# Routed attention and a hard-swish layer on one core: mask product in front, weight sums made earlier, loads issued later

## The chip, the core and the metric

The kernel runs on one core of one Trainium2 chip. The core has five engines that run side by side, each through its own list of instructions: TensorE (PE in the profile) for matrix products, VectorE (DVE), ScalarE (ACT) and GpSimd (POOL) for element-wise work, and SyncE (SP), which here only issues transfers. The metric is the device time of one execution in microseconds (us); the lower the better.

## The reference

Two layers follow one another. The first is attention in which a query sees only the keys of its own cluster; the second is a two-layer network with a hard-swish between.

```python
# q, k, v: (4, 8, 768, 64) float32; centroids: (8, 16, 64)
q_assign = np.argmax(np.einsum('bhsd,hcd->bhsc', q_n, c_n), axis=-1)
k_assign = np.argmax(np.einsum('bhsd,hcd->bhsc', k_n, c_n), axis=-1)
mask = q_assign[:, :, :, None] == k_assign[:, :, None, :]
scores = scale * np.matmul(q, k.transpose(0, 1, 3, 2))
scores = np.where(mask, scores, -1000000000.0)
attn = softmax(scores); attn_out = np.matmul(attn, v)
# x: (4*768, 512), heads side by side
h = x @ w_in                      # w_in (512, 2048), float64
g = h * np.clip(h + 3.0, 0.0, 6.0) / 6.0
out = g @ w_out                   # w_out (2048, 512), float64
```

Here `q_n`, `k_n` and `c_n` are the rows divided by their lengths.

## The kernel before, in words

The kernel is one program with a hand-written order. Attention works on 16 pairs of heads (g = 0 to 15). A pair has 12 items: an item is one block of 128 keys (j = 0 to 5) against half of the queries (hf = 0 or 1). The number n counts items over all pairs, 192 in all, and `where(n)` gives pair, half and key block. The big loop steps n by two, so that a step r = 0, 2, ... 10 of a pair takes two items. Four pairs make a batch.

**Scores (lines 410 to 429).** The scores of an item lie in a PSUM tile `ps`, of which there are two. For each head t of the pair, one f32 product of keys and queries from `xf` uses 64 rows of the array, so the two heads run side by side on rows 0 to 63 and 64 to 127. Then a second product from `xm` adds the mask: `xm` holds the one-hot cluster vectors of queries and, times a large negative number, the complement for keys, in bf16, so that items of different clusters get a large negative score. `scores` writes the f32 product first and the mask product after it. ScalarE then takes the exponential into `ex` (line 434), GpSimd sums the keys (`acc`), and PE multiplies by the values (`pv`, line 467).

**Preparing the next pair.** During pair g the queries and keys of pair g + 1 are turned by PE (`turn`), assigned to clusters (`cluster_scores`, `route`), and the one-hot vectors turned into `xm` (`route_turn`). At step r = 6 the loop issues the loads of q and k of pair g + 2 and of v of pair g + 1 (lines 873 to 875), six transfers of 192 KB on the Sync queue. A transfer there is issued only after those in front of it.

**From one by one to four by four.** For the first 96 items every step does all its work alone. From item 96 on (`fours`) the scores of four items, or of two, are taken together, and at r = 2, 6 and 10 a batch of the second layer's items (`fill`) is taken off a list, mixed with the preparing of the next pair (lines 876 to 883).

**The second layer (`ffn_items`).** Its tokens come in 12 blocks of 256. A block has 8 items `up` (the first product, with two of the 16 column tiles of `w_in` each) and 7 items `down` (the second product, parts 0 to 6). The first block's `up` is done plainly (line 603). All other blocks do the first product by a Strassen-like scheme with seven smaller products instead of eight (`halved`, tiles `uX` and `uY`): it needs three sums of weight tiles, called `tx`, and changes one weight tile of `w_in_sb` in place. VectorE adds the parts up into `g_sb`. The second product uses the same scheme from the first block on, with its own sums T1 to T4.

**Where `tx` comes from (`first_sums`, line 560).** u counts the `up` items over all blocks. For the second block (u = 8 to 15) VectorE makes the sums by four subtractions of 128x256 elements and a transfer stores them in HBM as `td`. For all later blocks a transfer reads them back from `td`. There are three buffers for `tx`. The call is two items ahead: `up` item u calls `first_sums(u + 2)`; the sums for u = 8 and 9 are made in parts 5 and 6 of the first block's `down` (lines 714 and 715).

**The Sync queue** carries, in the order of the program, loads of q, k and v, stores of the attention's result `num` to `xd` (line 496, which waits for VectorE's division), loads of token blocks `xb`, stores to `td`, reads of `tx`, and stores of the output.

Of the kernel before, what the change touches and what calls it, by code (L numbers as in the profile page):

```python
# [8 lines left out]
F32 = mybir.dt.float32  # L9
# [3 lines left out]
ALU = mybir.AluOpType  # L13
# [103 lines left out]
def fast_path(ctx, tc, ok, q, k, v, centroids, moe_w_in, moe_w_out, out):  # L117
# [288 lines left out]
    def where(n):  # L406
        g, r = divmod(n, 2 * NCH)
        return (g, *divmod(r, NCH))

    def scores_qk(n):  # L410
        g, hf, j = where(n)
        st["ps", n] = psum_s.tile([P, 2, 512], F32, name="ps")
        scores_part(n, st["xf", g], True)

    def scores_part(n, x, first):
        g, hf, j = where(n)
        for t in range(2):
            r = slice(t * D, (t + 1) * D)
            nc.tensor.matmul(  # L419
                st["ps", n][:, t, 0:HALF], lhsT=x[r, NCH + j],  # L420
                rhs=x[r, hf * NHC : (hf + 1) * NHC], start=first,
                stop=not first or by_vector(n),
            )

    def scores(n):
        if ("ps", n) not in st:
            scores_qk(n)
        if not by_vector(n):
            scores_part(n, st["xm", where(n)[0]], False)

    def exponentials(n):
        sc = st.pop(("ps", n))[:, :, 0:HALF]
# [127 lines left out]
    def first_sums(u):  # L560

        blk, i = divmod(u, HF)
        if not 0 < blk < B * NHC:
            return
        tx = st["tx", u] = txp.tile([P, 3, HK, P], F32, name="tx")
        if blk == 1:
            t1, t2, t4 = (tx[:, k] for k in range(3))
            b11, b12, b21, b22 = wi(0, 0, i), wi(0, 1, i), wi(1, 0, i), wi(1, 1, i)
            for out_, in0, in1 in ((t1, b12, b11), (t2, b22, t1), (t4, b21, t2), (b12, b22, b12)):
                nc.vector.tensor_tensor(out=out_, in0=in0, in1=in1, op=ALU.subtract)  # L570
            nc.sync.dma_start(td[:, i], tx)
        else:
            nc.sync.dma_start(tx, td[:, i])

    def token_sums(b, m):

# [15 lines left out]
    def ffn_items(b):  # L592
        def up(m, i):
            def item():
                load_block()
                u = (b * NHC + m) * HF + i
                g = g_sb[:, 0:4, i]
                if u < HF:
                    ph = psum_m.tile([P, 512], F32, name="ph", tag="m")
                    for t in range(2):  # L600
                        f = t * HF + i
                        for kt in range(NKT):
                            nc.tensor.matmul(  # L603
                                ph[:, t * HC : (t + 1) * HC], lhsT=w_in_sb[:, kt, f * P : (f + 1) * P],
                                rhs=st["xb", b, m][:, kt], start=(kt == 0), stop=(kt == NKT - 1),
                            )
                    ph = ph.rearrange("p (k c) -> p k c", k=4)
                    lift(g, ph)
                    clip(g, g, ph)
                    gated_sums(i)  # L610
                else:
                    halved(b, m, u, i, g)
                if u >= HF or i < HF - 2:
                    first_sums(u + 2)
                if i == HF - 1:
                    st.pop(("xb", b, m)), st.pop(("xs", b, m), None)
                    st["free"] = True
                    load_block()
                    finish()

            return item
# [70 lines left out]
        def down(m, part):  # L692
            def item():
                if part == 0:
                    st["X"] = psum_m.tile([P, DM], F32, name="X", tag="m")
                    st["y0"] = yp.tile([P, DM], F32, name="y0", tag="y0")
                elif part == 2:
                    st["Y"] = psum_m.tile([P, DM], F32, name="Y", tag="m")
                    st["y1"] = yp.tile([P, DM], F32, name="y1", tag="y1")

                if part < 2:
                    h = range(part * HF // 2, (part + 1) * HF // 2)
                    product(st["X"], 0, 0, wb[0][0], True, False, False, h)
                    product(st["X"], 1, 5, st["T2"], False, True, False, h)
                kind, bank, half, w = (
                    None, None,
                    (4, "Y", 0, st["T1"]), (1, "Y", 1, st["T3"]),
                    (2, "X", 0, wb[1][0]), (6, "Y", 0, wb[1][1]), (3, "Y", 1, st["T4"]),
                )[part] or (None,) * 4
                if part > 1:  # L710
                    product(st[bank], half, kind, w, part == 2, part in (3, 4, 6), part > 3)
                if part == 4:
                    token_sums(*divmod(b * NHC + m + 1, NHC))
                if (b, m) == (0, 0) and part > 4:
                    first_sums(HF + part - 5)
                y0, y1 = st["y0"], st.get("y1")
                if part == 1:
                    nc.scalar.copy(out=y0[:, HC:], in_=st["X"][:, HC:])
                    add(y0[:, HC:], y0[:, HC:], st["X"][:, 0:HC])
                elif part == 3:  # L720
                    add(y1[:, 0:HC], y0[:, HC:], st["Y"][:, HC:])
                    add(y1[:, HC:], y1[:, 0:HC], st["Y"][:, 0:HC])
                elif part == 4:
                    nc.scalar.copy(out=y0[:, 0:HC], in_=st["X"][:, 0:HC])
                elif part == 6:
                    add(y1[:, 0:HC], y0[:, HC:], st["Y"][:, HC:])
                    nc.sync.dma_start(out_v[b, 2 * m + 1], y1)
                    add(y0[:, HC:], y0[:, HC:], st["Y"][:, 0:HC])
                    nc.sync.dma_start(out_v[b, 2 * m], y0)

            return item
# [99 lines left out]
    with tc.manual_schedule():  # L831
        nc.scalar.dma_start(cen, centroids.rearrange("h c d -> (h c) d"))
        load(0, "q", "k")
        constants()
        load(0, "v")
        load_weights(0)
        centroid_norm()
        for part in range(3):
            turn(0, part)
        centroid_turn()  # L840
        nc.vector.tensor_copy(out=ident_q, in_=ident)
        load(1, "q", "k")
        cluster_scores(0)
        scores_qk(0)
        route(0)
        scores_qk(1)
        for part in range(2):
            route_turn(0, part)

        for n in range(0, total + lag_d + 2, 2):  # L850
            g, r = divmod(n, per_pair)
            fours = n >= DECODED
            steps = [i for i in (n, n + 1) if i < total]
            prep = prep_items(g + 1, r, fours)
            if fours:
                four_by_four(n, r, steps)
            else:
                for i in steps:
                    scores(i)
                    exponentials(i)  # L860
                    key_sums(i)
                for i in (n - lag_v, n - lag_v + 1):
                    if i >= 0:
                        attn_v(i)
                m = n - lag_d + 1
                if m >= 0 and m % NCH == NCH - 1:
                    later.append(divide(m))
                    ready(m)
            if prep and r == (6 if fours else 4):
                prep.pop(0)()  # L870
            if n == DECODED:
                st["early"] = False
            if r == 6:
                load(g + 2, "q", "k")
                load(g + 1, "v")
            if not fours or r % 4 == 2 or n >= total:
                want = min(items_by(n + 2) - st["done"], len(fill))
                st["done"] += want
                for i in range(max(len(prep), want)):
                    if i < want:  # L880
                        fill.pop(0)()
                    if i < len(prep):
                        prep[i]()
            for step in decode[: share[r]]:
                step()
            del decode[: share[r]]
            if not fours:
                for op in numbers:
                    op()
                numbers.clear()  # L890
                check_all()
            checks.extend(later)
            later.clear()

        while checks:
            check_all()
            checks.extend(later)
            later.clear()
        st["last"] = True
        for item in fill:  # L900
            item()
# [385 lines left out]
```

## Time and profile before

| | |
|---|---|
| device time, median of 3 runs | 1033.52 us (1029.15 to 1035.98) |
| span of the profiled execution | 1024.4 us |
| exponentials, ACT, x192 | 148.4 us, 806 ns each |
| score products, PE, 768 records | 165.5 us of PE's time |
| mask products, PE, 384 records | 63.1 us of PE's time |
| reads of `tx`, x80, 384 KB each | 3.2 us from issue to landing |
| loads of q and of k, x32 each, 192 KB | 4.3 and 4.6 us from issue to landing |

The profile records every instruction of one execution. An f32 matmul shows as two records, so that the scores of an item are four records of `ps<-xf` and two of `ps<-xm`. Records of PE overlap, since the two heads run side by side and matmuls are pipelined: busy time is the union of the records, and what a group costs is read best from the distance between starts. A row of the timeline gives start, length, engine, line, operation, output and inputs, the shape, the count, and in brackets the idle time before it with what ended it. "PEld" is the loading of weights, "SPq" the Sync queue. A row of waits gives who waited for whom, the sum in us, how often, and the longest.

### The profile page before, as it was taken

What the parts mean: (1) busy time and instruction counts of PE and PEld (TensorE: products, weight loads), DVE (VectorE), ACT (ScalarE), POOL (GpSimd) and SP (SyncE); (2) the same over time, 40 slices, a digit from 0 to 9 for tenths busy, and PEclk for the clock granted to TensorE, in tenths of its full rate; (3) what the DMA queues carried; (4) which work ended last, traced back from release to release, by engine and by line L of the source; (5) the groups of instructions that cost most, each with busy time, mean ns of one, the idle gap of its engine ahead of it and who ended that gap; (6) DMA issues with size and microseconds to landing.
All of it is one profiled execution on the core that took longest, in us unless ns stands there. A gap on an engine that the chain in (4) does not pass through costs nothing.

```text
span 1024.4 us, 16727 instructions
## 1 busy us (share of the span) xinstructions
PE 997.8 (97%) x6560; PEld 738.4 (72%) x6560; DVE 562.8 (55%) x1085; ACT 390.0 (38%) x764; POOL 433.3 (42%) x363
## 2 busy tenths in 40 slices
PE   8999999999999999999999999999999999999996
PEld 4444445546778777778787777678787898999995
DVE  4899977868368245226336236227246272727270
ACT  6888876675233233233323333333223020202010
POOL 4777756766325426426415415524516230303030
PEclk9999999999999999999999999999999999999999
DMA  6355664532223222223224025023023051414120
GB/s 177 101 145 144 165 165 97 143 86 46 58 91 110 55 91 83 54 75 103 58 83 118 27 68 152 9 70 98 29 84 97 3 154 40 143 40 126 51 63 25
DMA packets 107176, 90.34 MB, mean 88 GB/s; under 512 B 78416, under 2 KB 88656, under 8 KB 107088
## 3 DMA queue, kind: packets, MB, share of 16 engines
q1 hardware_dynamic: 106944, 89.15, 31.1%
q8 instruction: 54, 0.88, 0.3%
q14 instruction: 34, 0.28, 0.1%
q10 hardware_dynamic: 144, 0.03, 0.0%
HBM read 73.43 MB, written 15.73 MB: 87 GB/s over the span
## 4 chain that ended last, share of the span: by engine, by line
PE 84%; ACT 4%; DVE 4%; DMA 4%; SPq 2%; issue 1%; POOL 0%; ACTq 0%; DVEq 0%; POOLq 0%
PE Y L683 16%; PE uY L648 14%; PE ps L419 12%; PE X L683 12%; PE uX L648 11%; PE pv L467 9%; PE ph L603 3%; SPq L195 2%; PE pd L488 2%; PE pqk L310 2%; DMA raw<-in_moe_w_in_dram 1%; ACT ex L434 1%; PE pcs L323 1%; DMA tx<-td 1%; DVE wunit L247 1%
## 5 line engine op out<-in xcount | busy, mean ns | idle before, releaser
L457 POOL TENSOR_TENSOR acc<-acc,ex 128x768 f32<-128x768 f32 x128 | 241.3, 1885 | 139.0 <-ACT ex L434 132.6
L638 POOL TENSOR_TENSOR g_sb<-g_sb 128x256 f32<-128x256 f32 x176 | 130.5, 763 | 325.9 <-DVE g_sb L519 322.5
L434 ACT ACTIVATE ex<-ps 128x768 f32<-128x768 f32 x192 | 148.4, 806 | 87.4 <-PE ps L419 75.3
L516 ACT ACTIVATE sx<-g_sb,half_c 128x512 f32<-128x512 f32 x88 | 63.5, 722 | 277.5 <-DVE g_sb L659 277.5
L419 PE MATMUL ps<-xf 64*128 64x384 f32 x768 | 165.5, 509 | 2.7 <-ACT ex L434 2.6
L467 PE MATMUL pv<-ex,vt 128*64 128x384 f32 x768 | 141.1, 496 | 0.0
L690 DVE TENSOR_TENSOR y<-y,Y 128x256 f32<-128x256 f32 x48 | 20.2, 421 | 175.5 <-PE Y L683 174.7
L467 PEld LDWEIGHTS pv<-ex,vt 128*64 128x64 f32 x768 | 48.7, 136 | 78.2 <-issue 70.0
L492 DVE RECIPROCAL rcp<-pd 128x384 f32<-128x384 f32 x32 | 81.8, 2556 | 41.4 <-PE pd L488 41.3
L419 PEld LDWEIGHTS ps<-xf 64*128 64x128 f32 x768 | 63.1, 186 | 53.1 <-issue 36.5
L454 POOL TENSOR_TENSOR acc<-ex 128x768 f32<-128x768 f32 x32 | 59.8, 1867 | 94.9 <-ACT ex L434 94.9
L648 PE MATMUL uX<-xb,w_in_sb 128*128 128x128 f32 x704 | 93.8, 277 | 0.0
L683 PE MATMUL X<-w_out_sb,g_sb 128*128 128x256 f32 x384 | 89.7, 381 | 0.0
L683 PE MATMUL Y<-T,g_sb 128*128 128x256 f32 x384 | 87.3, 380 | 0.0
L683 PE MATMUL Y<-w_out_sb,g_sb 128*128 128x256 f32 x384 | 87.2, 380 | 0.0
L648 PEld LDWEIGHTS uX<-xb,w_in_sb 128*128 128x128 f32 x704 | 86.5, 194 | 0.0
L683 PEld LDWEIGHTS X<-w_out_sb,g_sb 128*128 128x128 f32 x384 | 71.3, 190 | 12.6 <-issue 3.8
L683 PEld LDWEIGHTS Y<-T,g_sb 128*128 128x128 f32 x384 | 72.3, 190 | 11.1 <-issue 1.6
L683 PEld LDWEIGHTS Y<-w_out_sb,g_sb 128*128 128x128 f32 x384 | 72.2, 190 | 11.0 <-issue 1.6
L519 DVE SCALAR_TENSOR_TENSOR g_sb<-sx,g_sb 128x512 f32<-128x512 f32 x88 | 66.9, 764 | 1.0 <-ACT sx L516 0.9
L419 PE MATMUL ps<-xm 64*128 64x384 bf16 x384 | 63.1, 323 | 3.1 <-ACT xm L369 2.8
L659 DVE TENSOR_TENSOR g_sb<-uY,sx 128x128 f32<-128x128 f32 (+1 forms) x176 | 65.7, 414 | 0.1
(110 smaller groups left out, 1381.5 us busy)
## 6 DMA issues: line engine op xcount, KB each, us to landing
tx<-td SPq DMA_DIRECT2D x80, 384.0 KB, 3.2
raw<-in_moe_w_in_dram SPq DMA_DIRECT2D x16, 512.0 KB, 3.8
raw<-in_moe_w_out_dram SPq DMA_DIRECT2D x16, 512.0 KB, 3.7
qk<-in_q_dram SPq DMA_DIRECT2D x32, 192.0 KB, 4.3
qk<-in_k_dram SPq DMA_DIRECT2D x32, 192.0 KB, 4.6
vt<-in_v_dram SPq DMA_DIRECT2D x32, 192.0 KB, 4.2
xd<-num SPq DMA_DIRECT2D x32, 192.0 KB, 2.4
xb<-xd SPq DMA_DIRECT2D x12, 512.0 KB, 4.0
```

The source lines that it names most:

```text
L419: nc.tensor.matmul(st["ps", n][:, t, 0:HALF], lhsT=x[r, NCH + j], rhs=x[r, hf * NHC : (hf + 1) * NHC], start=first, stop=not first or by_v ...
L434: nc.scalar.activation(out=ex, in_=sc, func=ACT.Exp, scale=SM_SCALE)
L454: nc.gpsimd.tensor_tensor(out=acc, in0=st["ex", n - 1], in1=ex, op=ALU.add)
L457: nc.gpsimd.tensor_tensor(out=acc, in0=acc, in1=ex, op=ALU.add)
L467: nc.tensor.matmul(pv[t * D : (t + 1) * D], lhsT=vt[:, j, t], rhs=ex[:, t], start=(j == 0), stop=(j == NCH - 1),)
L492: nc.vector.reciprocal(out=rcp, in_=pd)
L516: nc.scalar.activation(out=r, in_=h, func=ACT.Relu, bias=half_c, scale=1.0 / 6.0)
L519: nc.vector.scalar_tensor_tensor(out=g, in0=r, scalar=1.0, in1=h, op0=ALU.min, op1=ALU.mult)
L638: eng.tensor_tensor(out=out_, in0=in0, in1=in1, op=op)
L648: nc.tensor.matmul(dst, lhsT=w[:, kt], rhs=x(kt), start=(kt == 0), stop=(kt == HK - 1))
L659: nc.vector.tensor_tensor(out=out_, in0=in0, in1=in1, op=ALU.add)
L683: nc.tensor.matmul(bank[:, half * HC : (half + 1) * HC], lhsT=g_sb[:, kind, i], rhs=w[:, i], start=(first and i == 0), stop=(last and i == ...
```

## The change

There are three edits. The mask product is put in front of the score product, for every item but the first of a pair, whose mask is the last thing made for it, and the two items whose score product is issued ahead at the kernel's start. The sums `tx` for the second block are all made beside the first block's second product: parts 0 to 6 of `down` make those of items 7 and 6, 5, 4, 3, 2, 0 and 1. All are stored in `td`; those of items 0 and 1 also stay in their buffers, and items 2 to 7 of the second block now read theirs from `td` like later blocks. From item 96 on the loads for the next pairs are issued behind the items of step r = 6 instead of in front of them. The aim is to keep PE from waiting for sums and their transfers, and to have the small product begin a group.

```diff
     def scores(n):
+        g, hf, j = where(n)
         if ("ps", n) not in st:
-            scores_qk(n)
+            if hf == j == 0 or by_vector(n):
+                scores_qk(n)
+            else:
+                st["ps", n] = psum_s.tile([P, 2, 512], F32, name="ps")
+                scores_part(n, st["xm", g], True, False)
+                scores_part(n, st["xf", g], False, True)
+                return
         if not by_vector(n):
-            scores_part(n, st["xm", where(n)[0]], False)
+            scores_part(n, st["xm", g], False, True)
...
     def first_sums(u):
         blk, i = divmod(u, HF)
-        if not 0 < blk < B * NHC:
-            return
-        tx = st["tx", u] = txp.tile([P, 3, HK, P], F32, name="tx")
-        if blk == 1:
-            t1, t2, t4 = (tx[:, k] for k in range(3))
-            b11, b12, b21, b22 = wi(0, 0, i), wi(0, 1, i), wi(1, 0, i), wi(1, 1, i)
-            for out_, in0, in1 in ((t1, b12, b11), (t2, b22, t1), (t4, b21, t2), (b12, b22, b12)):
-                nc.vector.tensor_tensor(out=out_, in0=in0, in1=in1, op=ALU.subtract)
-            nc.sync.dma_start(td[:, i], tx)
-        else:
+        if ("tx", u) not in st and 0 < blk < B * NHC:
+            tx = st["tx", u] = txp.tile([P, 3, HK, P], F32, name="tx")
             nc.sync.dma_start(tx, td[:, i])
+
+    def make_first_sums(i):
+        tx = txp.tile([P, 3, HK, P], F32, name="tx")
+        t1, t2, t4 = (tx[:, k] for k in range(3))
+        b11, b12, b21, b22 = wi(0, 0, i), wi(0, 1, i), wi(1, 0, i), wi(1, 1, i)
+        for out_, in0, in1 in ((t1, b12, b11), (t2, b22, t1), (t4, b21, t2), (b12, b22, b12)):
+            nc.vector.tensor_tensor(out=out_, in0=in0, in1=in1, op=ALU.subtract)
+        nc.sync.dma_start(td[:, i], tx)
+        if i < 2:
+            st["tx", HF + i] = tx
...
-                if u >= HF or i < HF - 2:
+                if u >= HF:
                     first_sums(u + 2)
...
-                if (b, m) == (0, 0) and part > 4:
-                    first_sums(HF + part - 5)
+                if (b, m) == (0, 0):
+                    for i in ([HF - 1, HF - 2], [5], [4], [3], [2], [0], [1])[part]:
+                        make_first_sums(i)
...
-            if r == 6:
+            if r == 6 and not fours:
                 load(g + 2, "q", "k")
                 load(g + 1, "v")
...
+            if r == 6 and fours:
+                load(g + 2, "q", "k")
+                load(g + 1, "v")
             for step in decode[: share[r]]:
```

## The prediction

> **What bounds the kernel now.** I read the page first: busy shares, then the clock and the chain. PE is busy 997.8 of 1024.4 us, the chain that ended last is 84% PE, and every other engine is below 56%. An edit pays only if it shortens PE's own stream or takes away one of the few waits in it.
>
> ```profile
> span 1024.4 us, 16727 instructions
> PE 997.8 (97%) x6560; PEld 738.4 (72%) x6560; DVE 562.8 (55%) x1085; ACT 390.0 (38%) x764; POOL 433.3 (42%) x363
> PE 84%; ACT 4%; DVE 4%; DMA 4%; SPq 2%; issue 1%; POOL 0%; ACTq 0%; DVEq 0%; POOLq 0%
> ```
>
> Idle PE is 26.6 us. The table by stage tells where it lies (PE busy is the first number after the length):
>
> ```profile
> 0.00:110.00 110.00, 102.55 (x674) 47.65 (x676) 90.20 (x122) 88.59 (x189) 73.27 (x64) 1.00 0.57 147
> 110.00:250.00 140.00, 134.70 (x826) 70.62 (x823) 111.12 (x130) 98.58 (x216) 93.14 (x57) 1.00 0.43 117
> 250.00:777.00 527.00, 520.91 (x3480) 398.89 (x3476) 241.43 (x517) 169.09 (x304) 220.56 (x182) 1.00 0.26 74
> 777.00:1024.40 247.40, 239.65 (x1591) 221.25 (x1589) 120.09 (x319) 33.69 (x57) 46.38 (x63) 0.99 0.25 76
> ```
>
> The last stage is the tail behind the last product, the first holds the start. From 250 to 777 us, where the moved loads and sums work, PE idles 6.1 us. Two rows of PE's waits are nearly all of that:
>
> ```profile
> PE uX L648 <- DMA tx<-td: 3.8, 2, 2.3
> ...
> PE uX L648 <- DVE sx L659: 2.2, 3, 1.9
> ```
>
> Next the timeline of PE, once per kind of event (start, length, operation, idle before). First the second block's products: an undisturbed item (298.84), then one that waits.
>
> ```profile
> 298.84 0.66 PE L648 MATMUL uX<-xs,tx 128*128 128x128 f32 x4
> 302.02 0.50 PE L367 MATMUL po<-ident_q,one_hot 128*128 128x128 bf16 x6
> ...
> 307.99 1.03 PE L648 MATMUL uX<-xs,tx 128*128 128x128 f32 x4 [1.85 <-DVE sx L659]
> 308.81 1.91 PE L648 MATMUL uX<-xb,w_in_sb 128*128 128x128 f32 x8
> ...
> 312.84 0.61 PE L648 MATMUL uX<-xs,tx 128*128 128x128 f32 x4
> ```
>
> The undisturbed item lasts 3.18 us (298.84 to 302.02). The item at 307.99 lasts 4.85 us: after the wait its matmuls follow one another at twice the distance, so the wait of 1.85 us costs another 1.7 us. Then the Sync queue and PE around the longest transfer wait:
>
> ```profile
> 548.48 0.32 SPq L496 DMA_DIRECT2D xd<-num  x1
> 548.89 1.24 SPq L195 DMA_DIRECT2D qk<-in_q_dram  x2
> 550.18 1.33 SPq L195 DMA_DIRECT2D qk<-in_k_dram  x2
> 551.56 2.57 SPq L195 DMA_DIRECT2D vt<-in_v_dram  x2
> 554.23 1.94 SPq L573 DMA_DIRECT2D tx<-td  x3
> ...
> 558.57 0.68 PE L648 MATMUL uX<-xs,tx 128*128 128x128 f32 x4 [2.31 <-DMA tx<-td]
> ```
>
> Six issues for the next pair hold the queue for 5.3 us, and the sums that PE needs next stand behind them. Last, the scores, where no wait is named:
>
> ```profile
> 320.80 0.92 PE L419 MATMUL ps<-xf 64*128 64x384 f32 x4
> 321.55 0.33 PE L419 MATMUL ps<-xm 64*128 64x384 bf16 x2
> 321.71 0.81 PE L419 MATMUL ps<-xf 64*128 64x384 f32 x4
> 322.36 0.33 PE L419 MATMUL ps<-xm 64*128 64x384 bf16 x2
> ```
>
> The reader is to see 0.75 us from the first score product to its mask product, and 0.65 us from the second one to its own. Those are the same four matmul records. The first follows products that use the array in another shape (here the value product, 128*64), the second follows the mask product, which has the same shape (64*128). So 0.10 us is lost at each change of shape into an f32 product.
>
> **What the Trainium skill says.** TensorEngine Tiling (Array Packing), Key Properties: a change of tiling mode drains the array. The trace agrees: the last value product before a change keeps PE about 0.1 us longer (0.42 instead of 0.32 us to the next start). TensorE: Matmul & The Clock Gate, LDWEIGHTS: a load of 128 columns takes about 107 ns by its formula. That is the 104 ns which the first f32 product after a change lasts longer (587 against 482 ns). The same page, Weight-path perf modes: weights of 128 columns that are not FP32 load faster, about 2 times measured and 4 in theory. The trace of before shows a mask product that started after a wait, with its weights loaded only then, nine times: 333 ns against 322, so 11 ns exposed. The same page, Part 1, says the array's clock falls back after idle time; the trace shows the doubled distances after 307.99 and a granted clock of 0.96 in that stage, against 1.00 in the stages beside it.
>
> **The change part by part.**
>
> *Mask product in front.* Nothing is added or removed on PE; two groups swap. Before, a pair of items runs: change, score, mask, score, mask, change. After: change, mask, score, mask, score, change. The drain at either end stays. The weight load behind the drain is now that of the bf16 mask product (11 ns exposed) instead of the f32 one (104 ns). The f32 weights that follow load while the mask product streams; that already works between the items (score starts 0.16 us after mask, the mask's own length). Saving: 104 - 11 = 93 ns each. Counted in the timeline, 97 of the 192 score groups do not follow a mask product; the 16 first ones of a pair and the second of the kernel keep their order, which leaves 80. 80 x 93 ns = 7.4 us. If the fast load gains only the skill's measured factor 2, 53 ns stay exposed and the saving is 80 x 51 = 4.1 us; I take 93 because the nine waits show it on this tile. Up to about 110 us the chain runs through weight DMA, DVE and ACT, so part of it is lost there: some 24 of the pairs, half of 2.2 us, -1.1 us.
>
> *Sums beside the second product.* The 8 x 4 DVE subtractions of 0.42 us are the same; 24 of them leave the second block's first product, where DVE had 2.4 us of other work per item (0.29 + 0.62 + 0.29 + 0.74 + 0.68, overlapping a little) plus 1.7 to 4.8 us of sums against PE's 3.2 us. Without them DVE keeps up, as in the later blocks, which show this wait once, with 0.16 us. Gain: 1.85 + 1.7 us at 307.99 and 0.23 us at 302.75: 3.8 us. They move to 250 to 280 us, where from 251 to 266 DVE is busy 4.2 of 15 us. Six sets of 1.7 us are 10 us, and the set made in part 4 lies between 274.2 and 278.2, where DVE waited for PE. The last two, in parts 5 and 6, stay where they were. Hidden: PE is in 3.5 us parts there and waits only for the reciprocal at 269, before which DVE is idle 1.75 us. Added: six reads of td for items 2 to 7 of that block. Each waits for a buffer to come free, and behind it on the Sync queue stand other reads and the next pair's loads. It is issued when item i-3 is done, two items of 3.2 us ahead of its use, and lands in 3.2 us (median of the issues): hidden. The added stores' wait in the queue is for DVE; behind them stands only a store of num that was made later anyway.
>
> *Loads behind the items.* Same transfers, issued later. At 548 us the read of tx can then go at 548.9 instead of 554.2, lands by about 553, and PE needs it at 556.2: 2.31 us wait and 0.24 us slow matmuls after it go. At 623 us likewise (issue about 618.7 instead of 623.1, needed at 626.1): 1.44 + 0.24 us. Sum 4.2 us. The loads themselves now wait behind reads of tx; they are needed at step 2 of the next pair, at least 20 us later, and land in 4.6 us. Nothing waits for that.
>
> Sum: 7.4 - 1.1 + 3.8 + 4.2 = 14.3 us. From the median: 1033.5 - 14.3 = 1019.2, say 1019 us.
>
> **The rivals.**
>
> *1. The order of the products gives nothing.* The 64-row tiles could still expose the f32 load, because the mask product of 160 ns is too short after a drain, where both loads start together. For it: an f32 load record lasts 186 ns. Against it: between the items that load also starts with the mask product and is hidden. Then 8.0 us come from the waits: 1033.5 - 8.0 = 1025.5 us.
>
> *2. The waits move.* The order gives 6.3 us, but the removed waits return as waits for td in the second block, or for exponentials (PE already waits 8 times for ex). For it: only three tx buffers. Against it: later blocks read every tx that way and wait for two of 80 reads. 1033.5 - 7 = 1026.5 us.
>
> *3. Slower.* At each of the 80 pairs both loads are exposed and the drain lasts until the score product: +0.2 us each is +16 us, and the transfers still give their 8 us: about 1042 us. Against it: both neighbourhoods (mask to score, score to mask) exist in the trace and cost nothing.
>
> **How the numbers follow.** Chances: forecast 0.72, rival 1 0.10, rival 2 0.09, rival 3 0.09. The bound for 1% is 1023.2 us. The forecast falls under it in about 0.67 of its 0.72, and rival 2 in 0.03 (a partial return): faster 0.70. The rest of these and rival 1 are within 1%: 0.20. Rival 3: 0.10 rounded. Low end: all 15.4 us and the 3 us by which runs of before differ from their median, with a little for pairs I did not count: 1013. High end: rival 2 and a slow draw, 1028; rival 3 is left out.
>
> **What would show it.** Right: the score group is 0.65 us everywhere except at a pair's first item, the mask group after a change of shape lasts 0.17 us before the score begins; total busy of the score rows falls; no PE wait for tx or sx; reads of tx issued right behind the store of num. Wrong: score groups of 0.75 us behind the mask product; PE waiting for tx between 295 and 330 us; longer waits for ex, for rcp near 270 us, or for q and k at a pair's second step.

## The result, and the profile after

| | before | changed |
|---|---|---|
| device time, median of 4 runs each | 1033.33 us | 1015.83 us (1015.42 to 1018.16) |
| ratio, 95% interval | | 0.9839 [0.9803, 0.9875] |
| span of the profiled execution | 1024.4 us | 1013.6 us |

The kernel is 1.6% faster, 17.5 us by the medians, where 14.3 us were forecast. When both kernels were run again on another chip, the medians were 1028.71 and 1016.28 us, 12.4 us apart, the ratio 0.9865 [0.9836, 0.9895]. The two profiles differ by 10.8 us only. That gap is taken up below.

The page of the changed kernel: PE's share rises by a point, and of the chain that ended last DMA (4%) and the Sync queue (2%) are gone.

```profile
span 1013.6 us, 16743 instructions
PE 988.4 (98%) x6560; PEld 735.4 (73%) x6560; DVE 567.6 (56%) x1085; ACT 389.6 (38%) x764; POOL 431.6 (43%) x363
PE 82%; DVE 2%; ACT 1%; issue 0%; ACTq 0%
```

Its waits of PE (who waited for whom, us in all, times, longest) have no row for `tx<-td` any more; the wait for `sx` has shrunk from 2.2 to 1.1 us, and that for the exponentials has grown from 2.6 to 4.8 us (the first row is of before, the others are of the changed kernel). The 2.6 us are a low draw: other profiles with the old order show up to 4.2 us.

```profile
PE ps L419 <- ACT ex L434: 2.6, 8, 0.5
...
PE ps L418 <- ACT ex L441: 4.8, 9, 1.5
...
PE uX L658 <- DVE sx L669: 1.1, 3, 0.5
```

By stage (PE busy is the first number after the length), PE idles 1.1 us from 250 to 777 us, where it was 6.1 us. Before 250 us it idles 16.5 us, where it was 12.8 us. The second change is as much a part of the result as the first:

```profile
0.00:110.00 110.00, 99.76 (x668) 47.46 (x670) 91.34 (x121) 87.11 (x187) 71.59 (x64) 1.00 0.57 144
110.00:250.00 140.00, 133.75 (x832) 71.01 (x830) 112.40 (x131) 99.72 (x218) 93.73 (x57) 1.00 0.45 119
250.00:777.00 527.00, 525.93 (x3570) 406.24 (x3567) 251.44 (x537) 172.72 (x311) 223.14 (x186) 1.00 0.30 81
```

The timeline of PE at the scores of the second block (start, length, what ran), the place that the prediction shows of before at 320.80 us. First the first two items of a pair, which keep score before mask at the first, then the next step:

```profile
311.51 0.92 PE L418 MATMUL ps<-xf 64*128 64x384 f32 x4
312.26 0.49 PE L418 MATMUL ps<-xm 64*128 64x384 bf16 x4
...
316.06 0.34 PE L418 MATMUL ps<-xm 64*128 64x384 bf16 x2
316.24 0.81 PE L418 MATMUL ps<-xf 64*128 64x384 f32 x4
316.88 0.33 PE L418 MATMUL ps<-xm 64*128 64x384 bf16 x2
317.05 0.81 PE L418 MATMUL ps<-xf 64*128 64x384 f32 x4
317.78 0.49 PE L658 MATMUL uX<-xs,tx 128*128 128x128 f32 x2
```

At 311.51 the score product meets the change of shape and takes 0.75 us to the next start. At 316.06 the mask product meets it: 0.18 us, and both scores behind masks are short (0.64 us to the next mask; the last one, 0.73 us, ends in the drain, the 0.1 us that a change of shape costs and that was there before). From 316.06 to 317.78 the step takes 1.72 us; the same one took 1.82 us before.

The rows of weight loads show where the 0.1 us goes. In before (first row) the load of the score's f32 weights starts only with the product that needs it. Now the shorter load of the mask's weights stands there, and the score's load runs beside the mask product:

```profile
320.80 0.30 PEld L419 LDWEIGHTS ps<-xf 64*128 64x128 f32 x4 [0.76 <-ACT ex L434]
...
316.06 0.10 PEld L418 LDWEIGHTS <-xm 64*128 64x128 bf16 x2 [0.60 <-issue]
316.07 0.36 PEld L418 LDWEIGHTS ps<-xf 64*128 64x128 f32 x4
```

### The profile page after: what moved, and what is told of

The parts are those of the page before. It is cut to its first block, busy times and chain, and to the rows that moved or that the text cites. A ratio compares the mean times of both kernels' runs of the same rounds, so it can differ in the third digit from the quotient of the medians.

```text
span 1013.6 us, 16743 instructions
## 1 busy us (share of the span) xinstructions
PE 988.4 (98%) x6560; PEld 735.4 (73%) x6560; DVE 567.6 (56%) x1085; ACT 389.6 (38%) x764; POOL 431.6 (43%) x363
## 4 chain that ended last, share of the span: by engine, by line
PE 82%; DVE 2%; ACT 1%; issue 0%; ACTq 0%
PE Y L693 17%; PE uY L658 15%; PE X L693 12%; PE uX L658 12%; PE ps L418 11%; PE pv L474 9%; PE ph L613 3%; PE pd L495 2%; PE pqk L310 1%; PE pcs L323 1%; PE po L367 1%; ACT g_sb L523 0%; ACT xm L369 0%; DVE sx L669 0%; DVE g_sb L526 0%
## 5 line engine op out<-in xcount | busy, mean ns | idle before, releaser
L523 ACT ACTIVATE sx<-g_sb,half_c 128x512 f32<-128x512 f32 x88 | 63.6, 722 | 268.3 <-DVE g_sb L669 268.3
L418 PE MATMUL ps<-xf 64*128 64x384 f32 x768 | 157.1, 487 | 0.9 <-ACT ex L441 0.9
L418 PEld LDWEIGHTS ps<-xf 64*128 64x128 f32 x768 | 67.8, 188 | 21.1 <-issue 17.5
L418 PE MATMUL ps<-xm 64*128 64x384 bf16 x384 | 61.0, 327 | 7.4 <-ACT ex L441 4.0
```

Source lines behind the costliest of these rows:

```text
L418: nc.tensor.matmul(st["ps", n][:, t, 0:HALF], lhsT=x[r, NCH + j], rhs=x[r, hf * NHC : (hf + 1) * NHC], start=first, stop=last,)
L523: nc.scalar.activation(out=r, in_=h, func=ACT.Relu, bias=half_c, scale=1.0 / 6.0)
```

## The experiments

The tables of stages come from the timelines: each stage runs between the starts of the first value product (`pv`) of the items named. Item 96 is where steps are taken four by four; the second block's first product lies between 96 and 108, the two reads of `tx` that PE waited for between 144 and 180.

| us | to item 0 | 0 to 48 | 48 to 96 | 96 to 108 | 108 to 144 | 144 to 191 |
|---|---|---|---|---|---|---|
| before, first profile | 17.37 | 101.80 | 149.65 | 70.98 | 204.33 | 251.22 |
| before, second profile | 19.85 | 101.74 | 151.75 | 70.99 | 204.33 | 253.11 |
| order alone | 17.53 | 102.97 | 147.95 | 69.46 | 202.92 | 251.69 |
| sums alone | 17.61 | 102.12 | 151.63 | 66.67 | 204.34 | 253.13 |
| loads alone | 19.75 | 102.24 | 151.52 | 70.99 | 204.33 | 248.05 |
| sums and loads | 17.71 | 102.07 | 149.62 | 66.67 | 204.34 | 248.20 |
| changed, first profile | 17.37 | 103.00 | 148.31 | 66.19 | 202.92 | 246.88 |
| changed, second profile | 19.87 | 102.75 | 148.58 | 66.19 | 202.92 | 246.90 |

From item 96 to 144 kernels with the same edits agree to 0.02 us. The stages before and the one behind vary from run to run, so small differences there are read from times.

In what follows, a saving in us that stands beside a ratio is that ratio applied to the median of the runs of before on the same chip (1030.29, 1030.83 and 1028.71 us on the three chips). The plain difference of the medians is 0.7 to 1.5 us smaller.

### The kernel before once more

No edit.

> The kernel before, unchanged, once more. The profile of before spans 1024.4 us, but its timed runs have a median of 1033.3 us, 7 us above the 1026.2 us of the profiled run; the changed kernel shows no such spread (1015.4 to 1018.2 us). Theory: in most runs of before PE waits longer or more often for the sums tx (two waits of 3.8 us in the first profile), so that this profile shows 3 or more waits for tx, and 6 to 12 us of them. Rival: the spread comes from elsewhere (the start, the weights' transfers in the first 110 us); then the waits for tx are again near 4 us and the first 110 us of the trace are longer. Time: ratio 1.00.

1030.23 us, ratio 1.000 [0.9986, 1.0015], span of the profile 1030.7 us. The theory fell: one wait is put down to `tx`, 2.3 us, and another of 1.7 us at the place of the second one, though put down to VectorE, was for the read of `tx`, too: it landed at 633.82 us, the products start at 633.95 (how that is told is said under the sums alone). That makes two waits and 4.0 us, about as in the first profile. The 6.3 us by which this profile is longer come from elsewhere: 2.5 us before item 0; 2.1 us from 48 to 96, where PE waits 1.3 us longer for exponentials and 0.65 us longer for the first token block; 1.9 us behind 144, where the products behind the longest wait for `tx` ran at half pace for a while (the item took 4.83 us, in the first profile 3.20 us). The first of these is seen in the timelines of PE. This run of before:

```profile
9.42 1.51 PE L323 MATMUL pcs<-xf,cnT 128*32 128x384 f32 x8 [0.47 <-DVE ident_q L841]
10.86 1.65 PE L419 MATMUL ps<-xf 64*128 64x384 f32 x4
```

and the profile shown with the prediction:

```profile
8.69 0.85 PE L323 MATMUL pcs<-xf,cnT 128*32 128x384 f32 x8 [0.47 <-DVE ident_q L841]
9.48 0.92 PE L419 MATMUL ps<-xf 64*128 64x384 f32 x4
```

The same products take almost twice as long: the array still streams at the low pace. In which of the two ways a run begins differs between runs of one kernel; the changed kernel was profiled in both (17.37 and 19.87 us to item 0). So the first profile of before was a lucky one, and the difference of 10.8 us between the first two profiles is too small a measure of the change.

### One edit at a time

**Order alone.**

```diff
-            scores_qk(n)
+            if hf == j == 0 or by_vector(n): scores_qk(n)
+            else: (xm product with start, then xf product with stop); return
```

> Only the order of the products is changed. Theory: 93 ns at each of 80 changes of shape leave PE's stream, but the half before item 96 is taken back by waits for exponentials, so the time falls by 3.5 to 4.5 us (ratio 0.996), and the mask group behind a change lasts 173 ns, the score group behind it 645 ns. Rival (as the prediction summed it): nearly all of the 7.4 us shows, ratio 0.993. Second rival: the order gives nothing alone, ratio 1.000.

1025.51 us, ratio 0.9947 [0.9932, 0.9961]: 5.5 us, by the interval 4.0 to 7.0. From item 108 to 144, three pairs, it is 204.33 - 202.92 = 1.41 us, so 0.47 us per pair of heads; five changes of shape by 93 ns are 0.465 us. Over eight pairs that is 3.7 us. The time lies between theory and first rival, and the interval takes in the theory's 0.996, so this run alone doesn't tell whether part of the first half shows.

**Sums alone.** `first_sums` and `make_first_sums` as in the change; order and loads as before.

> Only the sums are moved to the first block's second product. Theory: the wait of 1.85 us for VectorE in the second block and the slow matmuls behind it go, with the wait of 0.23 us: 3.8 to 4.3 us less (ratio 0.996). Rival: the reads of td that are added, standing behind the next pair's loads in the queue as in the kernel before, make PE wait for tx in the second block, so that less than 2 us is left (ratio over 0.998).

1028.74 us, ratio 0.9974 [0.9957, 0.9991]: 2.7 us, by the interval 0.9 to 4.4. The stage from 96 to 108 is 4.31 us shorter, in every kernel that has this edit and not the order; the time is the blunter measure here. Nothing waits for the added reads. But both waits behind the loads are there (its waits of PE):

```profile
PE uX L651 <- DMA tx<-td: 2.0, 1, 2.0
PE uX L651 <- DVE g_sb L519: 1.8, 1, 1.8
```

The second row names VectorE's `g_sb`, yet the read of `tx` for that item, too, was issued only behind six loads. The traces settle which of the two ended last. In every wait of PE for `sx` in the second layer, over all profiles, the products start 54 to 56 ns behind VectorE's end (550.19 and 550.24 us in the changed kernel). In every wait for `tx` they start 135 or 136 ns behind the landing of the read (558.43 and 558.57 us in the first profile of before). Here they start 123 ns behind `g_sb` and 135 ns behind the landing at 625.65 us: it was the read, and the loads' edit removes this wait, too (next run). Behind it the products ran at half pace:

```profile
625.78 0.68 PE L651 MATMUL uX<-xs,tx 128*128 128x128 f32 x4 [1.84 <-DVE g_sb L519]
626.30 1.86 PE L651 MATMUL uX<-xb,w_in_sb 128*128 128x128 f32 x8
```

Eight records take 1.86 us there, elsewhere 1.06 us.

**Loads alone.**

```diff
-            if r == 6:
+            if r == 6 and not fours:
                 load(g + 2, "q", "k"); load(g + 1, "v")
...
+            if r == 6 and fours:                     # behind the items
+                load(g + 2, "q", "k"); load(g + 1, "v")
```

> Only the loads are issued behind the items. Theory: the waits for tx go; in the first profile that is 4.2 us, less some 0.9 us of waits for VectorE that lie beneath, so at least 3 us, and as much as 8 to 10 us against the median of the kernel before if its spread comes from these waits (ratio 0.991 to 0.997). Rival: the waits for tx come back at other places because the reads still wait for buffers: under 1 us (ratio 0.999 or more).

1025.21 us, ratio 0.9942 [0.9926, 0.9958]: 6.0 us, by the interval 4.3 to 7.6. The stage from 144 to 191 is 248.05 us, against 251.22 and 253.11: 3.2 and 5.1 us less. By time it can't be told from the order alone (5.5 us). In the changed kernel the Sync queue and PE at the place of the longest wait now look like this:

```profile
542.23 0.32 SPq L503 DMA_DIRECT2D xd<-num  x1
542.65 7.07 SPq L572 DMA_DIRECT2D tx<-td  x3
...
553.80 1.32 SPq L195 DMA_DIRECT2D qk<-in_q_dram  x2
...
550.24 0.71 PE L658 MATMUL uX<-xs,tx 128*128 128x128 f32 x4 [0.42 <-DVE sx L669]
```

The read goes out 0.42 us behind the store of `num`, not 5.75 us. PE's wait is 0.42 us where it was 2.31 us, and it is for VectorE, which here works off a product of the hard-swish (`g_sb`) and a routing (`mx`, `one_hot`) before `sx`:

```profile
547.27 0.94 DVE L526 SCALAR_TENSOR_TENSOR g_sb<-sx,g_sb 128x512 f32<-128x512 f32 x1
548.14 0.55 DVE L337 TENSOR_REDUCE mx<-pr 128x24 f32<-128x384 f32 x1
548.72 0.62 DVE L343 TENSOR_TENSOR one_hot<-pr,mx 128x192 bf16<-128x192 f32 x2
549.25 0.28 DVE L676 COPY sx<-uX 128x128 f32<-128x128 f32 x1
```

### Two edits without the third

**Sums and loads, old order.**

> The changed kernel without the new order of the products: sums and loads moved, score product first. Theory: the two edits do not get in each other's way, and the wait for tx of 2.0 us which the sums alone brought back near 610 us is gone, since the loads no longer stand in front of it; time 9 to 11 us less than before (ratio 0.990). Rival: the gains only add as measured alone or less (0.9974 x 0.9942 = 0.9916 or more). No wait for tx in the trace, and groups of 0.75 us from score to mask behind each change of shape.

1022.83 us, ratio 0.9910 [0.9881, 0.9938]: 9.3 us. The theory's low end (9 us) and the sum of the two alone (8.7 us) are too close for the time to tell them apart. The waits for `tx` are gone, and the stages are those of the two edits (66.67 us to 0.01, 248.20 to 0.15 us): they don't get in each other's way.

### Which product meets the change of shape

**Mask in front at the first item of a step only.**

```diff
-            if hf == j == 0 or by_vector(n):
+            if hf == j == 0 or by_vector(n) or n % 2:
```

> The changed kernel, but of the two items of a step only the first has its mask product in front: mask, score, score, mask. Theory (what counts is which product meets the change of shape): the same time as the changed kernel, ratio to before 0.983 to 0.986; the mask group behind a change lasts 173 ns, the scores follow one another without loss. Rival (each item gains by its own order, for instance since its exponential can start earlier): half of the order's gain is lost, 2 to 3 us more than the changed kernel.

1017.50 us, ratio 0.9860 [0.9833, 0.9887]. Its timeline:

```profile
320.24 0.34 PE L418 MATMUL ps<-xm 64*128 64x384 bf16 x2
320.41 1.45 PE L418 MATMUL ps<-xf 64*128 64x384 f32 x8
321.70 0.33 PE L418 MATMUL ps<-xm 64*128 64x384 bf16 x2
321.96 0.38 PE L658 MATMUL uX<-xs,tx 128*128 128x128 f32 x1
```

**At the second item only.**

```diff
-            if hf == j == 0 or by_vector(n):
+            if hf == j == 0 or by_vector(n) or n % 2 == 0:
```

> The counterpart: only the second item of a step has its mask product in front: score, mask, mask, score. Theory: all of the order's gain is lost; the first score group of a step lasts 0.75 us again, and the time is that of the kernel with sums and loads moved alone, some 5 us more than the changed kernel. Rival: half of the gain stays.

1021.75 us, ratio 0.9904 [0.9876, 0.9931]. Its timeline:

```profile
319.52 0.92 PE L418 MATMUL ps<-xf 64*128 64x384 f32 x4
320.27 0.49 PE L418 MATMUL ps<-xm 64*128 64x384 bf16 x4
320.60 0.81 PE L418 MATMUL ps<-xf 64*128 64x384 f32 x4
321.34 0.71 PE L658 MATMUL uX<-xs,tx 128*128 128x128 f32 x4
```

The first takes 1.72 us per step as the full change does, the second 1.82 us as before. The stages agree: behind item 96 the first has 66.19, 202.92 and 246.88 us, the changed kernel's numbers, and the second has 66.67, 204.34 and 248.21, those of the old order. So the gain belongs to the product that meets a change of shape and not to the order within an item. Behind item 96 one swap per step does all of it.

### How much of the first half shows

**Mask in front from item 96 on only**, run twice, the second time beside the changed kernel.

```diff
-            if hf == j == 0 or by_vector(n):
+            if hf == j == 0 or by_vector(n) or n < DECODED:
```

> The changed kernel, with the mask product in front only from item 96 on. Theory: before item 96 waits for exponentials and for the weights take back most of the 3.7 us (the prediction left 2.6 us there; the first pair of traces shows only 0.1 us), so this kernel is 0 to 2.6 us slower than the changed one; near 0 if the absorption is complete. Rival: the full 3.7 us show, ratio to the changed kernel 1.0035.

1018.81 us, ratio 0.9875 [0.9848, 0.9902].

> The changed kernel with the mask product in front only from item 96 on, once more, now beside the changed kernel on the same chip. Theory: 1 to 3 us slower than it, since part of the first half's 3.7 us shows and part is taken back by waits for exponentials (the prediction took 2.6 us). Rival: complete absorption, same time within 0.5 us. Second rival: 3.7 us slower.

> The changed kernel, unchanged, to stand beside the next three on one chip. Ratio to before 0.984 to 0.986. In its profile the steps from item 96 on repeat to 0.02 us; what differs between runs lies before: the cold array at the start (0 or 2.5 us) and the wait for the first token block (0 to 2 us).

On that chip: 1018.07 us (ratio to before 0.9891 [0.9861, 0.9921]) against the changed kernel's 1016.28 us (0.9865 [0.9836, 0.9895]). The medians differ by 1.8 us and the ratios by 2.7 us, though the intervals overlap. The stages to item 96 point the same way, 102.23 + 151.52 us here and 102.75 + 148.58 us in the changed kernel's second profile, 2.4 us, but they alone don't show it: with the old order their sum ranges from 251.45 to 253.76 us in the table, and the kernel with the mask in front at the first item of a step, which should gain as much as the changed kernel, took 102.55 + 150.59 = 253.14 us. So roughly half of 3.7 us shows, and its size is known to a us or so at best.

What takes the rest back is seen from item 0 to 48, which the order even lengthens by some 0.9 us. There PE waits 1.5 to 2.1 us for exponentials and 0.6 us for the cluster vectors (`one_hot`) in the five profiles of the table with the old order, and 3.5 to 3.7 us and 1.3 us in the three with the new one. What shows lies between 48 and 96.

**Three buffers for the weights' chunks, on top of the change.**

```diff
-    rawp = ...tile_pool(name="rawp", bufs=2)
+    rawp = ...tile_pool(name="rawp", bufs=3)
-            load_weights(i + 1)
+            load_weights(i + 2)      # and chunk 1 is read at the start
```

> The changed kernel with three buffers instead of two for the weights' raw chunks, each read two chunks ahead. Theory: in the first half ScalarE stands in line behind chunks of weights whose read could not be issued before VectorE had freed a buffer (0.8, 1.7 and 2.8 us of such waits from 79 to 108 us in the changed kernel's trace), and PE waits for its exponentials; with a third buffer these waits go, PE's idle time before item 96 falls by 2 to 4 us, and so does the time (ratio to the changed kernel 0.996 to 0.998). Rival: VectorE, busy 91 of the first 110 us, sets the pace, and nothing moves (within 0.5 us).

1017.24 us, ratio to before 0.9871 [0.9842, 0.9901]: nothing gained. ScalarE's waits for chunks, 7.3 us in the changed kernel beside it,

```profile
ACT wsize L221 <- DMA raw<-in_moe_w_in_dram: 6.7, 5, 2.6
ACT wsize L221 <- DMA raw<-in_moe_w_out_dram: 0.6, 1, 0.6
```

have no row in this kernel's waits, and the stage from 0 to 48 falls to 99.56 us, 3.2 us less. But the next stage grows from 148.58 to 154.07 us. PE waits 3.6 us for exponentials in it, where it was 1.2 us, and 3.0 us for the first token block, where it was 1.75 us; the longest ones:

```profile
129.94 0.34 PE L418 MATMUL ps<-xm 64*128 64x384 bf16 x2 [2.60 <-ACT ex L441]
144.55 5.38 PE L613 MATMUL ph<-xb,w_in_sb 128*128 128x256 f32 x16 [3.00 <-DMA xb<-xd]
```

The theory's mechanism was right and its gain wrong: the waits for chunks are real, but what is saved there PE spends at the next meeting point, and a wait of 3.00 us is followed by products at a lower pace (5.38 us instead of 3.69 in the changed kernel). In the next kernel, which has the third buffer too, the stages are 99.63 and 151.52 us: again what the first gains the second loses. What sets the pace of the first half, VectorE's decoding or the Sync queue, isn't settled by this run.

**The former with earlier warming at the start.**

```diff
+        cold = startp.tile([P, P], F32, name="cold"); nc.vector.memset(cold, 0.0)
+        for i in range(24): nc.tensor.matmul(warm[:, i % 4], lhsT=cold, rhs=cold, ...)
-        for i in range(14): nc.tensor.transpose(out=warm[:, i % 4], in_=ident, identity=ident)
```

> The former, and the array's warming products at the start made of a tile of zeros that VectorE fills, so that they begin some 0.5 us earlier, with 24 products instead of 14. Theory: the runs in which the first products still stream at half pace (2.5 us later at item 0) become rarer, so the median falls by up to 1.5 us against the kernel with three buffers. Rival: zeros do not warm the array or the products only delay the first turns: 0 to 1 us slower, with records of 275 ns distance at the start of the trace.

1017.96 us, ratio to before 0.9886 [0.9856, 0.9916]: no gain. An f32 product is two records, so that the 24 warming products took 48 records and 7.8 us; the first turn of queries begins at 8.85 us, and item 0 stands at 20.04 us.

```profile
1.05 7.96 PE L270 MATMUL warm<-cold 128*128 128x128 f32 x48 [1.05 <-DVE cold L267]
8.85 1.04 PE L312 MATMUL pqk<-ident,qk 128*128 128x128 f32 x8
```

Products of zeros do bring the array to its full pace: the distance between its records falls from 213 to 112 ns near 5.9 us, 4.9 us behind the first of them. But the warming went on for 2.9 us after that and held up the turns of the queries, so that this run doesn't tell what a shorter one is worth. No version here beats the changed kernel.

## Why the prediction was right, point by point

- **The order of the products.** Right in kind and size: the mask group behind a change of shape lasts 173 ns (162 plus 11), the score group behind it 645 ns, and 93 ns by five changes by pair is the 0.47 us that the stages from item 96 to 144 show (0.48 us for the one pair to 108, 1.41 us for three). The two half swaps show which product counts; that the difference is the load of its weights is read from the traces. One support of it was chance: the prediction takes the 107 ns of its formula for a weight load for these 104 ns, but a load record of these weights lasts 183 to 187 ns. The 11 ns, on which the size rests, were measured. Rivals 1 and 3 fell with it. The busy time of the score rows fell from 165.5 to 157.1 us, as it should.
- **What the first half takes back.** The term "half of 2.2 us, -1.1 us" was too small. It counted only the pairs up to 110 us, and of these only half. Some 2 of the first half's 3.7 us show, so about 2 us are lost: from item 0 to 48 PE's waits for exponentials grow by some 1.6 us and those for the cluster vectors by 0.7 us. Longer waits for exponentials were among the prediction's signs of being wrong and belong to rival 2; they came, but for a small part of the sum.
- **The sums.** 3.8 us were forecast, 4.31 us measured; the wait and the slow products behind it are gone. The added reads were hidden as forecast: no wait for `tx` in the second block. The step on the place they moved to was right with less room than stated. VectorE was still at the second layer's own sums until 254.8 us, and the first set then took 6.8 us instead of the 1.7 us of the sum:

```profile
254.83 0.94 DVE L580 TENSOR_TENSOR tx<-w_in_sb 128x256 f32<-128x256 f32 x1
255.80 3.87 DVE L580 TENSOR_TENSOR tx<-w_in_sb,tx 128x256 f32<-128x256 f32 x2
259.59 2.03 DVE L580 TENSOR_TENSOR w_in_sb<-w_in_sb 128x256 f32<-128x256 f32 x1
261.54 0.41 DVE L580 TENSOR_TENSOR tx<-w_in_sb 128x256 f32<-128x256 f32 x1
...
267.88 0.42 DVE L580 TENSOR_TENSOR w_in_sb<-w_in_sb 128x256 f32<-128x256 f32 x1
268.22 0.87 DVE L700 TENSOR_TENSOR y<-y,Y 128x256 f32<-128x256 f32 x2
269.01 2.55 DVE L499 RECIPROCAL rcp<-pd 128x384 f32<-128x384 f32 x1
```

  The five sets end at 268.3 us and the reciprocal starts at 269.01 us, where it started at 269.04 before. The 1.75 us of idle time that the prediction saw in front of it are used up. That it was just enough is luck.
- **The loads.** 4.2 us were forecast from the first profile; the stage lost 3.0 to 3.2 us against it. The step that was mis-sized is "1.44 + 0.24" and "2.31 us wait and 0.24 us slow matmuls after it go": beneath the waits for `tx` lay waits for VectorE, of which 0.42 and 0.49 us stayed. So the sign "no PE wait for tx or sx" came only in its first half. Against the second profile of before the stage lost 4.9 to 5.1 us, since there the products behind the longest wait ran at half pace.
- **The sum.** 14.3 us stand between 17.5 and 12.4 us, the two measurements. The one-edit kernels sum to 5.5 + 2.7 + 6.0 = 14.2 us by the ratios, but to 11.4 us by the medians. That the former agrees so well is luck: by stage the sums gave more than forecast (4.31 against 3.8 us), the order less, and by time the loads more than the first profile showed. From item 96 to 191 the changed kernel is 10.5 us shorter than the first profile of before and 12.4 us shorter than the second.

## What to carry to other kernels

Where products of different array shapes alternate, let the group behind each change begin with the product whose weights load fastest; nothing is added for it, and here one swap in two items gave all of it behind item 96. To tell what really ended a wait, compare the delay with that of clear cases. On a queue that issues in order, put transfers that are needed late behind those that are needed soon: here six issues for the next pair, in front of a read that PE waited for twice, cost 3 to 5 us by stage, about as much as the arithmetic that was moved (4.3 us). Judge a change of one percent by stages between the same instructions in both traces and by several runs, since one profile of this kernel can differ from the next by 6 us for reasons that no edit touches.

## What the runs showed of the hardware that was not expected

- The loss at a change of shape has two parts: a drain of about 0.10 us, which stays, and the exposed load of the first weights, 104 ns for 128 columns in f32 and 11 ns in bf16. The Trainium skill, TensorE: Matmul & The Clock Gate, Weight-path perf modes, gives a measured factor of about 2 for the load of 128 columns of weights that are not FP32. The load records agree with it (94 against 187 ns), yet the exposed part differs by a factor of 9. One reading fits: about 80 ns of a load that starts with its product stay hidden, whatever its length. The first load record behind a change exceeds the exposed part by 79 ns for f32 (183 less 104), by 82 ns for bf16 (93 less 11), and by 82 ns for the value product's f32 weights of 64 columns (133 less 51). This is an estimate from records of before and of the changed kernel; no run tests it.
- The start has two speeds. Of the profiles in the table, three reach item 0 at 19.75 to 19.87 us and five at 17.37 to 17.71 us.
- The same wait can leave different traces. At one place of the kernel before, the products behind 2.31 us of idle time lost 0.24 us in the first profile, and behind 2.34 us in the second some 15 of them started 213 instead of 112 ns apart, which cost 1.6 us. Behind the shorter wait of 1.85 us the first profile shows 3.4 us at half pace.
- A subtraction of 128x256 elements on VectorE took 0.41 to 0.43 us whenever no GpSimd instruction ran beside it for more than 0.05 us, in all fourteen profiles (22 to 26 of the 32 in each). Beside GpSimd one or two more were as fast, and the other five to eight took 0.83 to 2.04 us. In the changed kernel the slow ones were the four of the first set (0.94, 1.92, 1.92 and 2.03 us) and one more, and each ended 0.28 us behind the end of an addition on GpSimd (255.49, 257.44, 259.39, 261.34 and 276.03 us). No run takes the additions away.
